# Feed-forward matmuls that read their moving operand in turns from two halves 1 KB apart

## The chip, the cores and the metric

The kernel runs on one core of a Trainium2 chip. The metric is the device time of one execution in microseconds (us), the median of three runs. A core has five engines that work side by side on their own instruction streams and wait for each other through semaphores: TensorE (PE in the profile; its weight loads are shown apart as PEld), VectorE (DVE), ScalarE (ACT), GpSimd (POOL) and SyncE (SP), which here only starts DMA transfers. SBUF is the memory on the core that the engines read, 128 partitions wide; PSUM takes the results of TensorE.

A matmul has two operands. The stationary one (128 partitions by 128 columns here) is put into the array by a weight load of its own. The moving one (128 partitions by 512 columns) is then streamed past it, column by column, and 128 x 512 results are added up in one bank of PSUM. The access pattern of the moving operand says in which order its 512 columns are read.

## The reference

An attention over 8 batches, 8 heads, 576 positions and 64 channels, in two parts that are added: a local one (each position sees those fewer than 4 away) and one on q, k and v averaged over groups of 4 positions, repeated for the four. The sum is laid out as 4608 tokens of 512 channels and goes through a feed-forward block, which is nearly all of the arithmetic:

```
h = x @ w_in                                  # 4608 x 512 @ 512 x 2048
g = where(h >= 1, h, where(h <= -1, 0, (h + 1)**2 / 4))
out = g @ w_out                               # 4608 x 2048 @ 2048 x 512
```

## The kernel before

**Feed-forward.** All numbers are float32. TensorE multiplies them in a rounded form (float32r), so each factor is split into a high part, which is the rounded number, and a low part, which is the rest; a product is made of three matmuls: high x high, high x low, low x high. The tokens are worked off in 9 chunks `c` of 512, the 2048 inner channels in 16 slices `f` of 128.

- `mm1(c, f)` (line 455) makes one slice of h for one chunk: 4 blocks `cc` of 128 channels, three matmuls each, so 12. Stationary is a 128 x 128 block of `w_in` (`wi[:, wt, ...]`, `wt` 0 for the high part and 1 for the low), moving are 512 tokens of `xh` or `xl` (line 466). Its result `h_ps` has channels on the partitions and tokens along the row. ScalarE, VectorE and GpSimd then apply the function and split the result into `gh` and `gl` (lines 476 to 485).
- `mm2(c, f)` (line 488) multiplies `g` with `w_out`: for each of 4 tiles `t` of 128 tokens three matmuls, so again 12. Stationary are 128 tokens of `gh` or `gl`, moving is a row of 512 columns of `wo` (line 500). The four banks `o_ps` add up over the 16 slices; after the last, ScalarE copies each to `osb` (line 504), and SyncE starts the transfer of its 128 rows of 512 floats to `out` (line 505).

There are 9 x 16 pairs of `mm1` and `mm2`, so 144 x 24 = 3456 feed-forward matmuls.

**Attention.** 32 pairs of heads, each in pieces that are put between the feed-forward matmuls. It writes the tokens into `xh` and `xl` (lines 358 and 359), a ring of 3 x 512 tokens for each of the 4 channel blocks.

**Weights.** `w_in` and `w_out` arrive in 16 + 16 transfers as 64-bit words (line 369) and are turned into the high and low float32r parts by ScalarE, VectorE and GpSimd (lines 381 to 390). On the host, `w_out` is only reshaped to 16 x 128 x 512 (line 555).

**Order.** Two lists of steps (lines 79 and 83) set the order of the first stage; after that, attention pieces, `mm1` and `mm2` take turns in a loop (line 511).

Of the kernel before, what the change touches and what calls it, by code (L numbers as in the profile page):

```python
# [17 lines left out]
P = 128  # L18
# [4 lines left out]
DM = H * D  # L23
# [3 lines left out]
NFC = DFF // P  # L27
TCH = 512
# [72 lines left out]
def attention_then_ffn(ctx: ExitStack, tc, qT, kT, vw, vp, band, w_in, w_out, out):  # L101
    nc = tc.nc
# [269 lines left out]
    def temp(name):  # L372
        return mpool.tile([P, 512], F32, name=name, tag="t512", bufs=4)
# [34 lines left out]
    def emit(op):  # L408
        kind, n = op[0], int(op[1:] or 0)
        if kind == "a":  # L410
            if n not in attentions:
                attentions[n] = attention(n, rot if n < NPAIR else ps_a)
            next(attentions[n], None)
        elif kind == "c":
            convert_weights(*next(todo["c"]))
        elif kind == "w":
            load_weights(next(todo["w"]))
        elif kind == "q":
            nc.sync.dma_start(qk[n][0], qT[0, n])
            nc.sync.dma_start(qk[n][1], kT[0, n])  # L420
        elif kind == "v":
            load(0, "vp")
            load(0, "v")
        elif kind == "s":
            mm1(*next(todo["s"]))
        elif kind == "m":
            mm2(*next(todo["m"]))
# [24 lines left out]
    gtiles = {}  # L452
    otiles = {}

    def mm1(c, f):
        r0 = (c % 3) * TCH
        ts = slice(r0, r0 + TCH)
        wi = weights["i", f]
        h = ps_h.tile([P, 512], F32, name="h_ps", tag="h")
        n = 0  # L460
        for cc in range(NCC):
            for wt, xt in ((0, xh), (1, xh), (0, xl)):
                nc.tensor.matmul(  # L463
                    h[:, :TCH],
                    wi[:, wt, cc * P : (cc + 1) * P],
                    xt[:, cc, ts],
                    start=(n == 0),
                    stop=(n == 3 * NCC - 1),
                )
                n += 1  # L470
        with tc.high_priority(offset=100):
            u = temp("u")[:, :TCH]


            if c == 0:
                nc.vector.tensor_scalar(u, h[:, :TCH], -1.0, 1.0, op0=ALU.max, op1=ALU.add)
                nc.scalar.activation(u, u, AF.Square, scale=0.5)
            else:
                nc.scalar.activation(u, h[:, :TCH], AF.Relu, bias=0.5, scale=0.5)  # L479
                nc.scalar.activation(u, u, AF.Square)  # L480
            nc.vector.scalar_tensor_tensor(u, h[:, :TCH], 1.0, u, op0=ALU.max, op1=ALU.min)  # L481
            gh = mpool.tile([P, TCH], F32R, name="gh", tag="gh", bufs=3)
            gl = mpool.tile([P, TCH], F32R, name="gl", tag="gl", bufs=3)
            nc.scalar.copy(gh, u)  # L484
            nc.gpsimd.tensor_tensor(gl, u, gh, op=ALU.subtract)  # L485
        gtiles[c, f] = gh, gl

    def mm2(c, f):
        gh, gl = gtiles.pop((c, f))
        if f == 0:  # L490
            otiles[c] = [
                ps_o.tile([P, 512], F32, name=f"o_ps{t}", tag=f"o{t}") for t in range(NTT)
            ]
        wo = weights["o", f]
        for t in range(NTT):
            o = otiles[c][t]
            ts = slice(t * P, (t + 1) * P)
            for n, (gt, wt) in enumerate(((gh, 0), (gh, 1), (gl, 0))):
                nc.tensor.matmul(  # L499
                    o, gt[:, ts], wo[:, wt, :], start=f == 0 and n == 0, stop=f == NFC - 1 and n == 2  # L500
                )
            if f == NFC - 1:
                osb = temp("osb")
                nc.scalar.copy(osb, o)
                nc.sync.dma_start(out[c * TCH + t * P : c * TCH + (t + 1) * P, :], osb)

    steps = [(c, f) for c in range(NCH) for f in range(NFC)]
    todo["s"], todo["m"] = iter(steps), iter(steps)
# [2 lines left out]
    for c, f in todo["s"]:  # L511

        attn_step(NPAIR * (c + 2))
        mm1(c, f)
        mm2(*next(todo["m"]))
    for c, f in todo["m"]:
        mm2(c, f)
# [52 lines left out]
```

## Time and profile before

| | |
|---|---|
| median of 3 runs | 996.58 us (995.63 to 997.15) |
| span of the profiled execution, first to last instruction | 993.5 us |
| what the median has beside that span | 3.1 us |
| PE busy | 965.2 us (97% of the span), 7036 instructions |
| PEld busy | 762.9 us (77%) |
| DVE, ACT, POOL busy | 382.5, 456.9, 369.4 us |
| DMA | 66.13 MB, mean 67 GB/s |

The profile gives the span of its own execution; its time from outside, as the runs are timed, is not recorded, so the 3.1 us are the difference to the median of other executions. Matmuls are pipelined: the record of one lasts some 390 ns and overlaps the next. What a matmul costs in a dense stream is therefore read from the distance between the starts of two that follow each other (the timeline), not from the mean of one in a group.

### The profile page before, as it was taken

To read this page: it belongs to the slowest core of one execution; us is meant where nothing else is said; L and a number is where in the kernel's file an instruction comes from. 1 tells how busy PE (TensorE), PEld (TensorE's weight loads), DVE (VectorE), ACT (ScalarE), POOL (GpSimd) and SP (SyncE) were. 2 spreads that over 40 slices of the span, in tenths; PEclk is the share of its full clock that TensorE was granted. 3 is DMA by queue.
4 is the path that set the end of the run, shared out by engine and by line. 5 is a ranking of instruction groups with operands and counts; after the bars stand their busy time and mean duration, and the time that the engine had idled before them with its cause. 6 is when DMAs were issued, how large, how long until landed. Compare 5 with 4: busy or idle time off the path is not lost.

```text
span 993.5 us, 16968 instructions
## 1 busy us (share of the span) xinstructions
PE 965.2 (97%) x7036; PEld 762.9 (77%) x7036; DVE 382.5 (39%) x644; ACT 456.9 (46%) x911; POOL 369.4 (37%) x309
## 2 busy tenths in 40 slices
PE   5699999999999999999999999999999999999998
PEld 4577777777777777777777777777777788888886
DVE  5877786333333333333333333333333311111110
ACT  4988444444454444444444345444444443334333
POOL 2547565343333333333333433333333322222222
PEclk8689999999999999999999999999999999999999
DMA  9685112111121112111211112111211010001001
GB/s 309 230 294 176 50 50 82 60 50 40 36 92 50 47 32 87 50 49 50 92 51 49 50 27 92 49 50 40 77 50 50 14 44 0 1 1 43 1 1 42
DMA packets 26524, 66.13 MB, mean 67 GB/s; under 512 B 3152, under 2 KB 3152, under 8 KB 26448
## 3 DMA queue, kind: packets, MB, share of 16 engines
q1 hardware_dynamic: 26448, 65.06, 20.1%
q8 instruction: 55, 0.90, 0.4%
q14 instruction: 21, 0.17, 0.1%
HBM read 55.61 MB, written 9.44 MB: 65 GB/s over the span
## 4 chain that ended last, share of the span: by engine, by line
PE 83%; issue 7%; POOL 3%; ACT 2%; DMA 2%; DVE 2%; SPq 0%; POOLq 0%; DVEq 0%; ACTq 0%
PE o_ps L499 36%; PE h_ps L463 36%; PE sl_ps L191 2%; PE pl_ps L324 2%; PE pl_ps L336 2%; PE tp_ps L292 2%; POOL gl L485 2%; PE sp_ps L226 2%; PE tl_ps L280 1%; DMA raw_i<-w_in 1%; DMA vp_sb<-vp 1%; DVE m L386 1%; DVE m L387 0%; ACT raw_i L381 0%; ACT w_i L389 0%
## 5 line engine op out<-in xcount | busy, mean ns | idle before, releaser
L463 PE MATMUL h_ps<-xh,w_i 128*128 128x512 f32 x1152 | 373.9, 402 | 0.0
L499 PE MATMUL o_ps<-w_o,gh 128*128 128x512 f32 x1152 | 360.1, 394 | 0.2
L485 POOL TENSOR_TENSOR gl<-u,gh 128x512 fp32r<-128x512 f32 x144 | 186.6, 1296 | 431.6 <-ACT gh L484 325.3
L481 DVE SCALAR_TENSOR_TENSOR u<-h_ps,u 128x512 f32<-128x512 f32 x144 | 99.5, 691 | 453.1 <-ACT u L480 450.3
L499 PEld LDWEIGHTS o_ps<-w_o,gh 128*128 128x128 f32 x1152 | 215.5, 188 | 48.9 <-ACT gh L484 1.0
L463 PEld LDWEIGHTS h_ps<-xh,w_i 128*128 128x128 f32 x1152 | 211.1, 188 | 48.1 <-issue 5.2
L499 PE MATMUL o_ps<-w_o,gl 128*128 128x512 f32 x576 | 229.4, 398 | 2.4 <-POOL gl L485 2.4
L463 PE MATMUL h_ps<-xl,w_i 128*128 128x512 f32 x576 | 226.8, 394 | 0.0
L479 ACT ACTIVATE u<-h_ps 128x512 f32<-128x512 f32 x128 | 76.3, 596 | 148.0 <-PE h_ps L463 148.0
L484 ACT CAST gh<-u 128x512 fp32r<-128x512 f32 x144 | 89.6, 622 | 104.7 <-DVE u L481 104.6
L499 PEld LDWEIGHTS o_ps<-w_o,gl 128*128 128x128 f32 x576 | 108.1, 188 | 33.0 <-issue 4.8
L463 PEld LDWEIGHTS h_ps<-xl,w_i 128*128 128x128 f32 x576 | 108.4, 188 | 24.0
L480 ACT ACTIVATE u<-u 128x512 f32<-128x512 f32 x128 | 80.9, 632 | 3.8
L273 POOL TENSOR_TENSOR vh<-vp_sb 72x512 f32<-72x512 f32 x28 | 36.4, 1301 | 102.0 <-ACT u L480 91.7
L218 ACT ACTIVATE sl<-sl 128x640 f32<-128x640 f32 x32 | 23.6, 737 | 105.3 <-POOL sl L217 105.3
L246 ACT ACTIVATE sp<-sp_ps,mxp 128x144 f32<-128x144 f32 x96 | 36.5, 380 | 35.2 <-DVE mxp L244 33.4
L359 POOL TENSOR_TENSOR xl<-x,xh 128x576 fp32r<-128x576 f32 (+2 forms) x40 | 47.4, 1192 | 6.3 <-ACT xh L358 6.2
L217 POOL TENSOR_TENSOR sl<-sl,mxl 128x640 f32<-128x640 f32 x28 | 35.5, 1268 | 31.1 <-DVE mxl L216 31.1
L284 ACT COPY al<-tl_ps 128x640 f32<-128x640 f32 x32 | 22.2, 694 | 52.1 <-PE tl_ps L280 52.1
L255 DVE TENSOR_REDUCE sp_ps<-sl 128x10 f32<-128x640 f32 x32 | 26.5, 827 | 42.8 <-ACT sp L246 42.8
L280 PE MATMUL tl_ps<-ident,sl 128*128 128x128 f32 x160 | 25.0, 290 | 15.2 <-DVE sl L258 15.2
L213 DVE TENSOR_TENSOR sl<-sl_ps,band_sb 128x640 f32<-128x640 f32 x28 | 23.1, 824 | 38.2 <-PE sl_ps L191 38.2
(67 smaller groups left out, 755.3 us busy)
## 6 DMA issues: line engine op xcount, KB each, us to landing
v_sb<-vw SPq DMA_DIRECT2D x32, 320.0 KB, 3.1
vp_sb<-vp SPq DMA_DIRECT2D x32, 288.0 KB
out<-osb SPq DMA_DIRECT2D x36, 256.0 KB, 2.2
raw_i<-w_in SPq DMA_DIRECT2D x16, 512.0 KB, 6.9
raw_o<-w_out SPq DMA_DIRECT2D x16, 512.0 KB, 7.7
q_sb<-qT SPq DMA_DIRECT2D x28, 288.0 KB, 2.9
k_sb<-kT SPq DMA_DIRECT2D x28, 288.0 KB, 8.8
first_i<-qT SPq DMA_DIRECT2D x4, 288.0 KB
```

Source lines behind the costliest of these rows:

```text
L217: nc.gpsimd.tensor_tensor(slf, slf, ml_n, op=ALU.subtract)
L246: nc.scalar.activation(sp[:, i], sp_v[:, i] if i < 2 else sp_w, AF.Exp, bias=mx[:, i : i + 1], scale=scale, accum_out=sums[:, NB + i : NB ...
L273: nc.gpsimd.tensor_tensor(vh, vpt[:, :, 0:2, :], vpt[:, :, 2:4, :], op=ALU.add)
L280: nc.tensor.transpose(tl_v[:, g * P : (g + 1) * P], sl[:, g].rearrange("p r c -> p (r c)"), ident)
L359: nc.gpsimd.tensor_tensor(xl[:, p, dst], x[:, part], xh[:, p, dst], op=ALU.subtract)
L463: nc.tensor.matmul(h[:, :TCH], wi[:, wt, cc * P : (cc + 1) * P], xt[:, cc, ts], start=(n == 0), stop=(n == 3 * NCC - 1),)
L479: nc.scalar.activation(u, h[:, :TCH], AF.Relu, bias=0.5, scale=0.5)
L480: nc.scalar.activation(u, u, AF.Square)
L481: nc.vector.scalar_tensor_tensor(u, h[:, :TCH], 1.0, u, op0=ALU.max, op1=ALU.min)
L484: nc.scalar.copy(gh, u)
L485: nc.gpsimd.tensor_tensor(gl, u, gh, op=ALU.subtract)
L499: nc.tensor.matmul(o, gt[:, ts], wo[:, wt, :], start=f == 0 and n == 0, stop=f == NFC - 1 and n == 2)
```

## The change

A helper `turns` takes a block of 512 columns as two halves of 256 and reads column 0 of the first half, column 0 of the second, column 1 of the first, column 1 of the second, and so on. A column is 4 bytes in each partition, so the two halves lie 1 KB apart. It is applied to the moving operand of both kinds of feed-forward matmul; the number of columns, the stationary operands and the results' places in PSUM are as before.

In `mm1`, the tokens thus come out of the matmul in turns from both halves of the chunk, and stay in that order through `u`, `gh` and `gl`. A tile of 128 rows of `o_ps` then holds 64 tokens of the first half and 64 of the second, and the transfer to `out` puts each row in its place. In `mm2` the columns of `w_out` are read in turns, and the host lays them out so that the results come in the right order.

```diff
+    def turns(x):
+
+        return x.rearrange("p (a b) -> p b a", a=2)
+
     def mm1(c, f):
...
                 nc.tensor.matmul(
                     h[:, :TCH],
                     wi[:, wt, cc * P : (cc + 1) * P],
-                    xt[:, cc, ts],
+                    turns(xt[:, cc, ts]),
                     start=(n == 0),
                     stop=(n == 3 * NCC - 1),
                 )
...
                 nc.tensor.matmul(
-                    o, gt[:, ts], wo[:, wt, :], start=f == 0 and n == 0, stop=f == NFC - 1 and n == 2
+                    o, gt[:, ts], turns(wo[:, wt, :]), start=f == 0 and n == 0, stop=f == NFC - 1 and n == 2
                 )
             if f == NFC - 1:
                 osb = temp("osb")
                 nc.scalar.copy(osb, o)
-                nc.sync.dma_start(out[c * TCH + t * P : c * TCH + (t + 1) * P, :], osb)
+                rows = out[c * TCH : (c + 1) * TCH, :].rearrange("(a b) d -> b a d", a=2)
+                nc.sync.dma_start(rows[t * P // 2 : (t + 1) * P // 2], osb)
...
-        "w_out": words(inputs["moe_w_out"]).reshape(NFC, P, DM),
+        "w_out": np.ascontiguousarray(
+            words(inputs["moe_w_out"]).reshape(NFC, P, DM // 2, 2).transpose(0, 1, 3, 2)
+        ).reshape(NFC, P, DM),
```

The instructions of every engine stand in the same order as before, and there are as many of each. Four lines are added ahead of `mm1`, so line 463 becomes 467 and line 499 becomes 503. Beside the matmuls' access patterns, only the form of the 36 output transfers differs. The rows below are from SyncE's order at the end of a chunk of tokens, with the change's row marked +:

```order
@@ -72,5 +72,5 @@
 L134 DMA q_sb<-qT 128x576
 L134 DMA k_sb<-kT 128x576
-L505 DMA out<-osb 128x512 x4
+L510 DMA out<-osb 64x2x512 x4
 L140 DMA v_sb<-vw 128x640
 L137 DMA vp_sb<-vp 72x1024
```

The four transfers stay in their place; each writes 64 pairs of rows, the two rows of a pair 256 rows apart in `out`, instead of 128 rows in a piece.

## The prediction

> **What bounds the kernel now.** I read the shares of the engines first, then the clock, then the windows, and last the distances between matmuls.
>
> ```profile
> PE 965.2 (97%) x7036; PEld 762.9 (77%) x7036; DVE 382.5 (39%) x644; ACT 456.9 (46%) x911; POOL 369.4 (37%) x309
> PEclk8689999999999999999999999999999999999999
> 0.00:50.00 50.00, 30.52 (x424) 24.25 (x424) 35.47 (x68) 33.21 (x76) 20.59 (x26) 0.74 0.78 270
> 50.00:100.00 50.00, 46.44 (x365) 35.30 (x364) 38.98 (x60) 41.67 (x83) 30.14 (x22) 0.92 0.66 232
> 100.00:150.00 50.00, 49.59 (x395) 39.01 (x395) 39.84 (x66) 24.18 (x49) 31.36 (x23) 1.00 0.17 50
> 150.00:200.00 50.00, 49.60 (x398) 38.93 (x397) 23.86 (x38) 22.79 (x44) 23.63 (x20) 1.00 0.22 70
> ...
> 300.00:400.00 100.00, 100.00 (x762) 78.69 (x762) 37.78 (x66) 44.87 (x92) 35.69 (x31) 1.00 0.18 57
> ```
>
> The second row is the granted clock of TensorE in 40 slices, and in the rows by window the columns are the window, its length, busy time of PE, PEld, DVE, ACT and POOL with counts, the granted clock, the DMA share and GB/s. From 100 us on the clock is full. TensorE is idle for 19.5 us in the first window, 3.6 in the second, 0.4 in each of the next two, and not at all between 300 and 400, where no other engine is busy half the time. So TensorE bounds the kernel nearly from end to end.
>
> A busy TensorE does not say what one matmul costs, since the records overlap. These are the groups of the feed-forward and the start times in a stretch without attention:
>
> ```profile
> L463 PE MATMUL h_ps<-xh,w_i 128*128 128x512 f32 x1152 | 373.9, 402 | 0.0
> L499 PE MATMUL o_ps<-w_o,gh 128*128 128x512 f32 x1152 | 360.1, 394 | 0.2
> L499 PE MATMUL o_ps<-w_o,gl 128*128 128x512 f32 x576 | 229.4, 398 | 2.4 <-POOL gl L485 2.4
> L463 PE MATMUL h_ps<-xl,w_i 128*128 128x512 f32 x576 | 226.8, 394 | 0.0
> ```
>
> ```profile
> 902.58 0.63 PE L463 MATMUL h_ps<-xh,w_i 128*128 128x512 f32 x2
> 903.05 0.39 PE L463 MATMUL h_ps<-xl,w_i 128*128 128x512 f32 x1
> ...
> 905.34 0.63 PE L499 MATMUL o_ps<-w_o,gh 128*128 128x512 f32 x2
> 905.81 0.40 PE L499 MATMUL o_ps<-w_o,gl 128*128 128x512 f32 x1
> ...
> 907.43 0.62 PE L499 MATMUL o_ps<-w_o,gh 128*128 128x512 f32 x2
> 907.88 0.39 PE L499 MATMUL o_ps<-w_o,gl 128*128 128x512 f32 x1
> 908.11 0.40 PE L463 MATMUL h_ps<-xh,w_i 128*128 128x512 f32 x1
> ```
>
> One `mm1` and one `mm2`, 24 matmuls, run from 902.58 to 908.11: 5.53 us, 230.4 ns from start to start, 0.45 ns a column. Two starting at 905.34 take 0.47 us, two at 907.43 take 0.45, so steps lie between 225 and 235 ns. The groups count 1152 + 1152 + 576 + 576 = 3456 matmuls; at 230.4 ns they are 796 us of the 993.5 us span. A nanosecond more on each is 3.5 us on the end.
>
> Each has a weight load of its own, and that is not what paces them:
>
> ```profile
> L463 PEld LDWEIGHTS h_ps<-xh,w_i 128*128 128x128 f32 x1152 | 211.1, 188 | 48.1 <-issue 5.2
> ```
>
> ```profile
> 608.20 0.71 PE L280 MATMUL tl_ps<-ident,sl 128*128 128x128 f32 x5
> 608.66 0.71 PE L463 MATMUL h_ps<-xh,w_i 128*128 128x512 f32 x2
> ```
>
> A load lasts 188 ns, 42 less than a step. In the attention, five matmuls of 128 columns with loads of the same size go from 608.20 to 608.66, 92 ns each by these merged starts. So loads can follow far faster than every 230 ns, and the 512 moving columns fill the step. What their reading costs more is paid in full.
>
> **The change part by part.** No instruction is added, removed or moved. Three things are different.
>
> (1) *The moving read of 3456 matmuls.* Before, neighbouring columns are read one after the other. Now each read is 1 KB from the one before, and none follows its neighbour. No matmul of the trace reads like this, so I bound the price. The nearest row is on another engine: line 268 adds up groups of four numbers that lie 512 bytes apart, lines 166, 242 and 243 reduce numbers that lie side by side.
>
> ```profile
> L268 DVE TENSOR_REDUCE vd<-vp_sb 72x256 f32<-72x1024 f32 x4 | 8.1, 2017 | 1.1 <-DMA vp_sb<-vp 0.8 <-PE pl_ps L336 0.3
> L166 DVE TENSOR_REDUCE first_qd<-q_sb 128x144 f32<-128x576 f32 x28 | 20.8, 741 | 0.3 <-DMA q_sb<-qT 0.3
> L242 DVE TENSOR_REDUCE sp_ps<-sp_ps 128x1 f32<-128x144 f32 x32 | 10.0, 313 | 14.5 <-PE sp_ps L226 14.5
> L243 DVE TENSOR_REDUCE sp_ps<-sp_ps 128x2 f32<-128x288 f32 x32 | 14.6, 456 | 0.1
> ```
>
> From 144 to 288 numbers the time grows by 143 ns, 0.99 ns each, with 170 ns fixed. Line 166, groups of four side by side, fits: (741 - 170) / 576 = 0.99. Line 268 gives (2017 - 170) / 1024 = 1.80 ns. Reading in turns from four places cost VectorE 0.81 ns a number, 0.82 of its own time for one.
>
> From below, the price on TensorE is nothing, or a gain; those are rivals. Where there is a stall, I scale it by the engine's own pace. The step of 225 ns is the most that streaming alone can be, since steps that short occur. At 0.82 of it a matmul costs 184 ns more; at a whole further column time for each column, 225 ns more. I take 213 ns, nearer the upper end: in line 268 each number still has a sum of four to close, in which a stall may hide, while a matmul has nothing between its columns. So 3456 x 213 = 736 us.
>
> [...]
>
> (2) *The order of columns and rows.* ScalarE, VectorE and GpSimd work on `u`, `gh` and `gl` element by element; the token order costs them nothing. `w_out` is laid out on the host, and its transfers are as large and as contiguous as before.
>
> (3) *The 36 output transfers.*
>
> ```profile
> out<-osb SPq DMA_DIRECT2D x36, 256.0 KB, 2.2
> ```
>
> Each still moves 128 rows of 2 KB and lands 2.2 us after its issue. All but the last lie under the matmuls. If the scattered rows doubled a landing, the end would come 2.2 us later; I count 0.
>
> *What takes some of it back.* A slower stream waits less for others. TensorE's idle time from 50 to 200 us is 4.4 us, and the groups show 2.4 us of waiting for `gl`. The first 19.5 us lie ahead of the feed-forward and stay. I count 4 us back. No engine becomes a bound: per feed-forward matmul all have the same work in nearly twice the time. As PE never rests, I expect the clock to stay full.
>
> *Sum.* The span of 993.5 becomes 993.5 + 736 - 4 = 1725.5, and with the 3.1 us that the median has beside it 1728.6: **1729 us**. With 184 and 225 instead of 213 it is 1629 and 1770, so the own range of this case is 1620 to 1780.
>
> **The rivals.**
>
> *No change (17%).* If the read addresses run far enough ahead of the array, a read elsewhere costs as little as a neighbour. For it: ScalarE reads every second word in line 381 at little extra over line 477, which reads all.
>
> ```profile
> L381 ACT ACTIVATE raw_i<-raw_i 128x512 f32<-128x512 f32 x16 | 10.7, 668 | 13.0 <-DMA raw_i<-w_in 13.0
> L477 ACT ACTIVATE u<-u 128x512 f32<-128x512 f32 x16 | 10.1, 630 | 7.4 <-DVE u L476 7.4
> ```
>
> 668 against 630 ns is 6%. Against it: its step is 8 bytes and not 1 KB, and line 268, with 512 bytes, shows that the distance is felt. The time would be 996.6. The same would show if the pattern had no effect on how the columns are fetched. [...]
>
> *Faster (22%).* If neighbouring reads meet in one part of the memory, and turns between two parts keep them out of each other's way, the steps become shorter. For it: they differ by 10 ns, though all do the same. With all at the shortest, 225 ns, 3456 x 5.4 = 19 us go and the time is 978; with the 10 ns once more below that, 215 ns, it is 943. It decides as soon as the mean step falls below 229.8 ns (2 us). Against it: line 268, which also takes turns between places 1 KB apart, is slower and not faster.
>
> *A stall on some reads only (7%).* One kind of matmul, or a read in four, pays: from 736 / 4 = 184 us to 368 us more, 1180 to 1365.
>
> *A stall that lasts as long as VectorE's (4%).* 0.81 ns on each of 512 columns is 415 ns a matmul and 1434 us in all: about 2430.
>
> **How the numbers follow.** The stall of nearly one column time has 50%, partial stalls 7%, the long one 4%: slower 61%. A measurement of this kernel can tell about 0.2% (2 us) from no change; the second rival lies inside that, 17%; faster 22%. The predicted time is that of the likeliest case, 1729 us. Cases of both signs hold most of the chance, so the range reaches from 950, into the faster case, to 1780, the likeliest case's upper end; it leaves out the long stall and the ends of the two. Between 1365 and 1620 I expect next to nothing.
>
> **What would show it.** Right: start to start of the matmuls at lines 467 and 503 near 443 ns on the timeline, in `mm1` and `mm2` alike; about 10.6 us for a pair of them where it was 5.53; PEld's share falling from 77% to near 45% with its loads still 188 ns; waits for `gl` gone; the attention matmuls unchanged; the granted clock still full. If `mm1` and `mm2` differ, the price hangs on what else lies in memory, not on the distance of 1 KB. Wrong: steps of 225 to 235 ns (no stall on TensorE, and VectorE's row was no guide), or steps under 225 (the reads were in each other's way before). If the steps double but the time does not, it was not TensorE that set the end. An output transfer that lands much later than 2.2 us would show the third part as mispriced.

## The result and the profile after

The changed kernel takes 954.36 us (median of 4 runs, 953.24 to 955.23), the kernel before 996.21 beside it. The ratio is 0.9577, 95% interval 0.9563 to 0.959: 4.2% faster, where 1729 us were predicted. The span of the profiled execution is 952.7 us, 40.8 less than before.

From the page of the changed kernel, shares of the engines, granted clock, and output transfers (KB each, us to landing):

```profile
PE 920.8 (97%) x7036; PEld 767.9 (81%) x7036; DVE 384.4 (40%) x644; ACT 459.4 (48%) x911; POOL 368.2 (39%) x309
PEclk7579999999999999999999999999999999999999
out<-osb SPq DMA_DIRECT2D x36, 256.0 KB, 2.5
```

The counts are those of before. TensorE is as busy as ever (97% of the span), its clock as full after the first slices (9 tenths or more), and the other engines have the same work. The transfers to `out` land 0.3 us later than the 2.2 of before. What changed is how fast matmuls follow each other. The timeline of the changed kernel, one `mm2` and one `mm1` (start, us, then the group):

```profile
900.22 0.59 PE L503 MATMUL o_ps<-w_o,gh 128*128 128x512 f32 x2
900.65 0.38 PE L503 MATMUL o_ps<-w_o,gl 128*128 128x512 f32 x1
...
902.80 0.59 PE L467 MATMUL h_ps<-xh,w_i 128*128 128x512 f32 x2
903.24 0.38 PE L467 MATMUL h_ps<-xl,w_i 128*128 128x512 f32 x1
...
905.39 0.59 PE L503 MATMUL o_ps<-w_o,gh 128*128 128x512 f32 x2
```

24 matmuls take 5.17 us where they took 5.53. Over all starts in the trace (steps next to attention left out) the mean step is 215.9 ns in both kinds, and in the dense stretch of the last two chunks nearly every one is 215 or 216. Before, the mean was 230.3 in `mm1` and 230.8 in `mm2`, and single steps went from 224 to 237 in a pattern that came back in each slice. Such means from the trace's starts are given for all runs below.

3456 x 14.7 ns would be 50.8 us; 40.8 arrived. The starts of `mm1` for each chunk say where the rest is. The first chunk begins at 55.9 us before and at 55.7 after, and then takes 109.7 us before and 111.6 after: it gained nothing. Chunks 1 to 6 take 5.3 us less each, chunks 7 and 8, which have no attention beside them, 5.6, which is 384 x 14.7 ns; from the start of the last matmul to the end of the span it takes 4.8 us instead of 4.3. In the windows of the first stage (window, length, busy PE, PEld, DVE, ACT, POOL, granted clock, DMA share, GB/s) of the changed kernel

```profile
50.00:100.00 50.00, 43.62 (x348) 33.93 (x347) 37.75 (x59) 45.41 (x82) 28.41 (x21) 0.88 0.65 230
100.00:150.00 50.00, 48.75 (x404) 40.00 (x403) 41.20 (x64) 23.62 (x47) 32.99 (x25) 1.00 0.17 50
150.00:200.00 50.00, 49.14 (x406) 40.35 (x405) 25.74 (x42) 23.61 (x47) 24.08 (x21) 1.00 0.22 70
```

TensorE idles 8.5 us between 50 and 200 us, where it idled 4.4, and the clock in the first of them is 0.88 instead of 0.92. In this stage the other engines convert weights and prepare attention; TensorE got to its waits sooner. That is read from the rows; no run changed this stage. The later traces agree with it: within the first chunk TensorE idles 2.9 us before, 5.0 with one kind of matmul turned, and 6.4 to 8.1 with both, and in none of them does the chunk take less than 109.7 us. The lower clock is not what they share: the changed kernel run again has 0.93 between 50 and 100 us, and its first chunk takes 111.7.

### The profile page after: what moved, and what is told of

Its sections match the earlier page's. It is cut to its first block, busy times and chain, and to the rows that moved or that the text cites. A ratio compares the mean times of both kernels' runs of the same rounds, so it can differ in the third digit from the quotient of the medians.

```text
span 952.7 us, 16968 instructions
## 1 busy us (share of the span) xinstructions
PE 920.8 (97%) x7036; PEld 767.9 (81%) x7036; DVE 384.4 (40%) x644; ACT 459.4 (48%) x911; POOL 368.2 (39%) x309
## 4 chain that ended last, share of the span: by engine, by line
PE 81%; issue 6%; ACT 5%; DVE 4%; POOL 2%; DMA 2%; SPq 0%; POOLq 0%; ACTq 0%; DVEq 0%
PE h_ps L467 34%; PE o_ps L503 34%; PE sl_ps L191 3%; PE pl_ps L324 2%; PE tp_ps L292 2%; PE pl_ps L336 2%; PE sp_ps L226 2%; PE tl_ps L280 2%; POOL gl L489 2%; DVE m L387 1%; DVE m L386 1%; ACT sp L246 1%; DMA raw_o<-w_out 1%; ACT raw_i L383 1%; ACT raw_i L381 1%
## 5 line engine op out<-in xcount | busy, mean ns | idle before, releaser
L467 PE MATMUL h_ps<-xh,w_i 128*128 128x512 f32 x1152 | 357.6, 388 | 0.1
L503 PE MATMUL o_ps<-w_o,gh 128*128 128x512 f32 x1152 | 345.2, 381 | 1.4 <-ACT gh L488 1.4
L503 PE MATMUL o_ps<-w_o,gl 128*128 128x512 f32 x576 | 222.1, 386 | 3.6 <-POOL gl L489 3.6
L467 PE MATMUL h_ps<-xl,w_i 128*128 128x512 f32 x576 | 218.8, 380 | 0.0
L467 PEld LDWEIGHTS h_ps<-xl,w_i 128*128 128x128 f32 x576 | 109.1, 189 | 14.7
L280 PEld LDWEIGHTS tl_ps<-ident,sl 128*128 128x128 f32 x160 | 19.5, 150 | 22.1 <-issue 13.3
```

The source lines that it names most:

```text
L280: nc.tensor.transpose(tl_v[:, g * P : (g + 1) * P], sl[:, g].rearrange("p r c -> p (r c)"), ident)
L467: nc.tensor.matmul(h[:, :TCH], wi[:, wt, cc * P : (cc + 1) * P], turns(xt[:, cc, ts]), start=(n == 0), stop=(n == 3 * NCC - 1),)
L503: nc.tensor.matmul(o, gt[:, ts], turns(wo[:, wt, :]), start=f == 0 and n == 0, stop=f == NFC - 1 and n == 2)
```

## The experiments

The question was why reading in turns is fast. Three theories: **parts**, two places far apart keep successive reads out of each other's way; **neighbours**, the straight read holds itself up by staying within a few bytes; **load**, the weight load of the next matmul and the straight read meet. My own theory, the lost turn (nearly a whole further column time for each column), was on the list too.

### One kind of matmul alone

`e1_mm1_only` keeps `turns` in `mm1` and reads `w_out` as before; `e2_mm2_only` the other way round:

```diff
-                    o, gt[:, ts], turns(wo[:, wt, :]), start=...
+                    o, gt[:, ts], wo[:, wt, :], start=...          # e1
-                    turns(xt[:, cc, ts]),
+                    xt[:, cc, ts],                                  # e2
```

> Only the moving operand of mm1 is read in turns; mm2 reads its 512 columns one after the other, and w_out is laid out as before. If the step of each turned matmul falls from 230.5 to 215.9 ns whatever stands beside it, mm1's 1728 matmuls bring 1728 x 14.6 = 25 us of 50, so about 21 of the 42 us measured: 975 us. If the two kinds disturb each other (a turned read helps the straight one behind it, or a straight one spoils the turned), the steps of mm2 fall below 230.8 ns too, or those of mm1 stay above 216, and the time is well off 975.

> Only the moving operand of mm2 is read in turns, with w_out laid out to match; mm1 and the output transfers are as before. Matmul by matmul: 975 us, steps of 215.9 ns in mm2 and 230.5 in mm1. The transfers' new form, if it costs anything, is missing here and there in the run with mm1 alone, so the two gains would add up to more than 42 us by that much.

Measured: 974.99 us, ratio 0.9793 (0.9774 to 0.9813), and 973.25 us, ratio 0.9778 (0.9763 to 0.9793). Timeline of the run with `mm1` alone:

```profile
851.13 0.61 PE L503 MATMUL o_ps<-w_o,gh 128*128 128x512 f32 x2
851.59 0.39 PE L503 MATMUL o_ps<-w_o,gl 128*128 128x512 f32 x1
...
852.49 0.59 PE L467 MATMUL h_ps<-xh,w_i 128*128 128x512 f32 x2
852.92 0.38 PE L467 MATMUL h_ps<-xl,w_i 128*128 128x512 f32 x1
```

Two straight matmuls take 0.46 us, two turned ones 0.43. In dense stretches the turned kind stands at 215.8 ns, the straight kind at 229 to 230. The gain belongs to each matmul by itself: 2.07% and 2.22% add up, within the intervals, to the 4.2% of both.

### Nine orders of the moving columns

`e3_scan_orders` gives each chunk of tokens another order, so that one run compares nine. This scan and the four like it are single runs; the steps are compared within the trace, not the times:

```diff
+    ORDERS = [
+        lambda x: x.rearrange("p (a b) -> p b a", a=2),             # chunk 0
+        lambda x: x,
+        lambda x: pairs_apart(x, 128), ... 64, 16, 4                # "p (x a b) -> p x b a", a=2
+        lambda x: x.rearrange("p (b a) -> p a b", a=2),             # 6
+        lambda x: x.rearrange("p (b a) -> p a b", a=4),
+        lambda x: x.rearrange("p (a b c) -> p b a c", a=2, c=4),    # 8
+    ]
```

> Each chunk of 512 tokens reads the moving operands of its 384 matmuls in another order (so the output is in a wrong order and partly a product of wrong columns; the work is the same). Chunk 0: turns 1 KB apart. 1: straight on. 2, 3, 4, 5: turns between places 512, 256, 64 and 16 bytes apart. 6: every second column, then the others (8 bytes apart). 7: every fourth (16 bytes apart). 8: four columns (16 bytes) from one half, then four from the other. Theory of parts (two places must lie in different parts of the memory, far apart): 215.9 ns in chunks 0 and 8 and from some distance on in 2 to 5; 230 ns or more in 1, 6, 7 and the short distances. Theory of neighbours (reads that stay within a few bytes hold each other up): 215.9 ns in 0, 2, 3, 4, 5 and 7, 230 in 1, something between in 6 and 8. Theory of the lost turn, which my prediction had (a read far from the last costs a further column time): 7 and 8 would be slower than 230.

The timeline of this run, a few rows each from chunk 1 (straight), 5 (turns 16 bytes apart), 6 (every second column) and 7 (every fourth):

```profile
200.56 0.62 PE L481 MATMUL h_ps<-xh,w_i 128*128 128x512 f32 x2
201.02 0.39 PE L481 MATMUL h_ps<-xl,w_i 128*128 128x512 f32 x1
...
640.38 0.59 PE L517 MATMUL o_ps<-w_o,gh 128*128 128x512 f32 x2
640.81 0.38 PE L517 MATMUL o_ps<-w_o,gl 128*128 128x512 f32 x1
...
741.08 1.09 PE L481 MATMUL h_ps<-xh,w_i 128*128 128x512 f32 x2
741.99 0.64 PE L481 MATMUL h_ps<-xl,w_i 128*128 128x512 f32 x1
...
920.95 1.10 PE L517 MATMUL o_ps<-w_o,gh 128*128 128x512 f32 x2
921.87 0.64 PE L517 MATMUL o_ps<-w_o,gl 128*128 128x512 f32 x1
```

Two steps take 0.46, 0.43, 0.91 and 0.92 us. Turns are at 215.8 to 216.1 ns at every distance, 16 bytes included: **parts** falls. Every fourth column, whose reads also lie 16 bytes apart, is at 460: **neighbours** falls as I had put it. And the lost turn exists: reading every second or fourth column costs 221 to 231 ns more than straight on. It does not come with turns.

### Sizes, loads and blocks

`e4_scan_forms` varies the operands' sizes by chunk:

```diff
+    FORMS = [(halves, P, TCH), (blocks(2), P, TCH), (blocks(16), P, TCH),
+        (lambda x: x[:, ::-1], P, TCH), (plain, P, 384), (halves, P, 384),
+        (plain, 72, TCH), (plain, P, TCH), (plain, 96, TCH)]
+        wgt = row[:, i::4] if c == 7 else row[:, i * P : (i + 1) * P]
```

> Again another form of the 384 matmuls in each chunk; after the first matmul of a sum, chunks 4 to 6 and 8 leave out part of the columns of one operand. Chunk 0: turns 1 KB apart, as control. 1 and 2: blocks of two and of 16 columns from the halves in turns. 3: straight on, but backwards. 4: 384 moving columns straight on. 5: 384 moving columns in turns. 6 and 8: straight on, with a stationary operand of 72 and of 96 columns instead of 128. 7: straight on, with a stationary operand whose columns lie 16 bytes apart. Theory of the load (the weight load of the next matmul and a straight moving read meet, 14.7 ns a matmul): the 14.7 ns shrink with the stationary columns, to 11 at 96 and 8 at 72 (steps of 227 and 224 ns), change in 7, and are the same 14 to 15 ns in 4 against 5. Theory of the read alone (the straight read holds itself up, whatever is loaded): 6, 7 and 8 stay at 230, and the difference of 4 and 5 is three quarters of 14.7, 11 ns. Backwards in 3: 230 if neighbours are what counts.

Weight loads of chunks 6 and 7, each from the groups of a window of that chunk (count, busy us, mean ns, idle):

```profile
L481 PEld LDWEIGHTS h_ps<-xh,w_i 128*72 128x72 f32 x64 | 9.0, 142 | 4.5
...
L481 PEld LDWEIGHTS h_ps<-xh,w_i 128*128 128x128 f32 x106 | 28.9, 308 | 0.0
```

With 72 stationary columns a load lasts 142 ns instead of 188, with columns 16 bytes apart 308; the steps are 231 to 233 ns with 72 columns, 231 to 234 with 96, 235 to 238 with the spread ones. A shorter load brings nothing, so **load** falls; a much longer one costs some 6 ns. With 384 moving columns in dense stretches, straight steps are 173 ns in `mm1` and 176 in `mm2`, turned ones 162.5 in both: 11 and 13 ns apart, where three quarters of 14.7 are 11. In `mm1` the loss thus goes with the number of columns read; in `mm2` it shrinks by less. Backwards: 233.6. Blocks from the two halves in turns are all slower than straight on: 334 ns with two columns, 240 with 16 (and 251 with four, in the run before).

### Two readers or kept lines

What turns of any distance have in common is that every second column of the order is a neighbour of the one two before. That led to the theory of two readers, one for even and one for odd positions in the order. No trace shows a reader; the theory is about the steps. `e5_scan_streams` tests orders in which it and its rivals part, and VectorE's row of my prediction beside it:

```diff
+    ORDERS = [halves, quarters, steps_of(2), steps_of(4),            # "p (a b e) -> p e b a", a=2
+        pairs_apart(x, 2), pairs swapped, 256 columns each twice, pairs_apart(x, 8), eighths]
-                vd, vpt.rearrange("k n f c -> k n c f"), axis=AX.X, op=ALU.add
+                dst, groups of four 512, 4, 16 or 8 bytes apart, axis=AX.X, op=ALU.add
```

> Another order of the moving columns in each chunk (the output is in a wrong order and partly a product of wrong columns). Chunk 0: halves in turns, as control. 1: quarters in turns (0, 128, 256, 384, 1, ...). 2: halves in turns, every second column of each (0, 256, 2, 258, ...), then the others. 3: the same with every fourth. 4: 0, 2, 1, 3, 4, 6, 5, 7, ... 5: neighbours swapped, 1, 0, 3, 2, ... 6: the first 256 columns, each twice in a row. 7: turns between places 32 bytes apart. 8: eighths in turns. Theory of two readers (even and odd columns are fetched by two readers, and each wants its next column in the 16 bytes it has just read; straight on, a reader finds two there, in turns four): 216 ns in 0, 6, 7; near 230 in 2, 4, 5, where each reader finds two; 330 to 460 in 1, 3, 8, where it finds one. Theory of kept lines (the last two or more 16-byte stretches are kept, and turns leave twice the time to fetch the next): 216 in 0, 6, 7 and, if four are kept, in 1; 230 in 4 and 5; 450 in 2, as where every second column was read straight on. Theory of 8-byte words: 216 in 4, 450 in 2. Beside it, line 268's reduction by VectorE takes its groups of four 512 bytes apart (as before), side by side, 16 bytes apart and 8 bytes apart, once each: if distance is what cost it 0.81 ns a number, 2.0, 1.2, 2.0 and 1.2 us.

Timeline, chunk 1 (quarters), 2 (halves, every second column), 3 (halves, every fourth), 6 (each column twice) and 8 (eighths):

```profile
220.68 0.73 PE L533 MATMUL o_ps<-w_o,gh 128*128 128x512 f32 x2
221.25 0.45 PE L533 MATMUL o_ps<-w_o,gl 128*128 128x512 f32 x1
...
340.44 0.62 PE L533 MATMUL o_ps<-w_o,gh 128*128 128x512 f32 x2
340.90 0.39 PE L533 MATMUL o_ps<-w_o,gl 128*128 128x512 f32 x1
...
480.18 1.08 PE L533 MATMUL o_ps<-w_o,gh 128*128 128x512 f32 x2
481.08 0.63 PE L533 MATMUL o_ps<-w_o,gl 128*128 128x512 f32 x1
...
870.60 0.59 PE L497 MATMUL h_ps<-xh,w_i 128*128 128x512 f32 x2
871.03 0.38 PE L497 MATMUL h_ps<-xl,w_i 128*128 128x512 f32 x1
...
1040.27 1.18 PE L497 MATMUL h_ps<-xh,w_i 128*128 128x512 f32 x2
1041.24 0.69 PE L497 MATMUL h_ps<-xl,w_i 128*128 128x512 f32 x1
```

All float32r orders of the runs together, sorted by how many successive reads of one reader fall into the same 16 bytes. The readers and the 16 bytes are the theory's assumptions; the steps are measured:

| order of the 512 columns | found together | step, ns (mm1 / mm2) |
|---|---|---|
| turns 1 KB, 512, 256, 64, 32 or 16 bytes apart | 4 | 215.8 to 216.2 |
| 256 columns, each twice | 4 | 215.8 / 215.8 |
| straight on | 2 | 230.2 / 230.6 |
| 0, 2, 1, 3, 4, 6, ... | 2 | 230.2 / 230.6 |
| neighbours swapped | 2 | 230.2 / 230.9 |
| halves in turns, every second column | 2 | 230.2 / 230.9 |
| backwards | 2 | 233.6 / 233.6 |
| blocks of 16; of 4 from the halves | 2 | 240.2 / 240.4; 249.9 / 251.9 |
| quarters in turns | 1 | 279.4 / 283.1 |
| blocks of 2 from the halves | 1 | 334.2 / 333.1 |
| every second; every fourth column | 1 | 454.3 / 451.8; 461.1 / 460.0 |
| halves in turns, every fourth column | 1 | 454.4 / 451.6 |
| eighths in turns | 1 | 487.5 / 487.5 |

Halves with every second column separate the theories. Kept lines and 8-byte words said 450; they are at 230 and repeat the pattern of straight steps (236, 235, 232, 232, 225, 230, ...). Halves with every fourth column are at 452 to 454, like every second column straight on. Each time it counts what lies at every second place of the order, not what lies next. **Two readers** sorts all fifteen into three classes without overlap. It does not give the sizes within a class: of the three orders forecast at 330 to 460, quarters came out below (279 to 283), eighths above (487). Quarters and blocks of two (334) come out cheaper than the other orders where a reader never finds two together. They alternate between two stretches a reader, eighths between four; so a stretch left for one read may still be at hand for the next. This stays open.

VectorE's four reductions in this run, with groups of four 512 bytes, 4, 16 and 8 bytes apart (start and us of each):

```profile
49.06 1.95 DVE L280 TENSOR_REDUCE vd<-vp_sb 72x256 f32<-72x1024 f32 x1 [1.05 <-PE tp_ps L302]
75.20 1.20 DVE L280 TENSOR_REDUCE vd<-vp_sb 72x256 f32<-72x1024 f32 x1
106.77 2.15 DVE L280 TENSOR_REDUCE vd<-vp_sb 72x256 f32<-72x1024 f32 x1
134.59 1.21 DVE L280 TENSOR_REDUCE vd<-vp_sb 72x256 f32<-72x1024 f32 x1
```

On VectorE distance does cost what I read from its row: 1.95 us at 512 bytes and 2.15 at 16, against 1.20 side by side. At 8 bytes it costs nothing (1.21 us), where on TensorE every second column, 8 bytes a step, doubles the time (452 to 454 ns against 230). TensorE's turns, at 16 bytes and more, are 14.7 ns a matmul faster than straight on.

### Other types of operand

`e6_scan_types` and `e9_scan_bf16` ask whether this carries over:

```diff
+    FORMS = [(halves, F32R), (plain, BF16), (halves, BF16), (every(2), BF16), (every(4), BF16),
+        (every(8), BF16), (every(16), BF16), (plain, F32), (halves, F32)]          # e6
+    FORMS = [(halves, F32R), plain, halves, each twice, blocks(2), apart(2), blocks(4),
+        apart(4), every(2), all BF16 with 256 columns]                             # e9
```

> Beside the first matmul of each sum, which stays as it was, chunks 1 to 6 use bfloat16 operands: one fixed stationary block and 256 fixed columns read twice (so the output is not the reference's), straight on in 1, halves (256 bytes apart) in turns in 2, every 2nd, 4th, 8th and 16th column in 3 to 6, which is 4, 8, 16 and 32 bytes from one to the next. Chunks 7 and 8 multiply the float32r tiles as plain float32, straight on and in turns; chunk 0 is in turns as control. By the theory of two readers a straight read of 2-byte columns finds four in each 16 bytes: 216 ns in 1 and 2, near 230 in 3, wait for each column (some 460) in 5 and 6, in 4 as well. By the theory of kept lines likewise 216 in 1 and 2, and 230 in 3. If only 4-byte operands are held up, 1 to 3 are alike. Plain float32 takes several passes; if a pass is slow enough for the reads, 7 and 8 are alike, and the attention's float32 matmuls have nothing to gain from turns.

> bfloat16 again, now 256 columns a matmul (one fixed stationary block and one fixed row of 256 columns beside the first matmul of each sum, so the output is not the reference's); straight on it should take half of 216, 108 to 110 ns. Chunk 1: straight on. 2: halves (256 bytes apart) in turns. 3: the first 128 columns, each twice. 4: blocks of two from the halves in turns. 5: 0, 2, 1, 3, ... 6: blocks of four from the halves. 7: 0, 4, 1, 5, ... 8: every second column, then the others. If two readers took even and odd columns here as well, 2, 3 and 7 would stand at 109; the 485 ns of the halves with 512 columns speaks against it. If the unit is a word of 4 bytes, two columns, then 4 takes the place of the turns (109) and 2, 3, 5 and 7, which break up the words, are slow (240). If a reader takes four columns at once from one 16-byte stretch, 1, 3, 5 and 6 are at 109 to 115, 2 and 4 near 240, 7 at 109 (eight neighbours in all), 8 at 113.

In the first, bfloat16 takes 216 ns straight on, 484 in turns of halves, 225 with every second column and 451 with every fourth. Every 8th and 16th are at 900 and 918, mostly at another clock. Windows of chunks 4, 5 and 6, then two short ones (the clock stands behind POOL), and matmuls of every 8th (`h_ps`) and every fourth column (`o_ps`) from there:

```profile
588.00:768.00 180.00, 180.00 (x794) 54.35 (x792) 36.23 (x60) 43.75 (x87) 38.45 (x35) 0.99 0.09 28
775.00:1130.00 355.00, 355.00 (x816) 72.34 (x816) 38.99 (x67) 45.67 (x90) 39.10 (x32) 0.51 0.05 15
1135.00:1500.00 365.00, 365.00 (x784) 74.28 (x783) 36.83 (x64) 47.27 (x94) 35.40 (x29) 0.50 0.03 11
...
764.00:774.00 10.00, 10.00 (x18) 2.08 (x17) 0.69 (x1) 2.60 (x5) 0.00 (x0) 0.50 0.07 26
774.00:780.00 6.00, 6.00 (x21) 1.26 (x20) 2.68 (x7) 2.71 (x9) 1.27 (x1) 1.00 0.35 131
```

```profile
759.54 10.06 PE L489 MATMUL h_ps<-half_x,ident 128*128 128x512 bf16 x11
769.42 5.59 PE L489 MATMUL o_ps<-half_x,ident 128*128 128x512 bf16 x12
...
775.92 10.06 PE L489 MATMUL h_ps<-half_x,ident 128*128 128x512 bf16 x11
```

The granted clock does not make these steps. Those of every 8th column take 900 ns at half clock and at full clock alike (from 776.80 to 780.40 us it is full), and the steps of every fourth from 769.42 us, at half clock, take 450 to 452 ns like those at full clock before. So at these two strides the steps took as long at half clock as at full. Columns 16 bytes apart cost bfloat16 900 ns, twice the 460 that they cost float32r, which no theory had forecast.

Plain float32 leaves two records for each matmul, here called passes. At the border of chunks 7 and 8, `mm1` (`h_ps`) already reads in turns and `mm2` (`o_ps`) still straight on:

```profile
1824.90 2.33 PE L498 MATMUL h_ps<-xh,w_i 128*128 128x512 f32 x4
1827.07 1.25 PE L498 MATMUL h_ps<-xl,w_i 128*128 128x512 f32 x2
1828.15 1.88 PE L498 MATMUL o_ps<-w_o,gh 128*128 128x512 f32 x4
1829.87 1.02 PE L498 MATMUL o_ps<-w_o,gl 128*128 128x512 f32 x2
```

A pass takes 429 ns straight on and 540 to 542 in turns, at full clock. Turns make plain float32 slower, by 111 to 113 ns a pass. That the attention's float32 matmuls would lose by them as well is my estimate from this; no run turned them.

In the second, with 256 columns, steps are 109 ns straight on, 109 with each column twice, with 0, 2, 1, 3 and with 0, 4, 1, 5; 113 with blocks of four and with every second column; 137 with blocks of two; 243 with halves. Rows from the straight order (chunk 1), the halves (chunk 2) and the blocks of two (chunk 4):

```profile
227.59 1.38 PE L492 MATMUL h_ps<-half_x,ident 128*128 128x256 bf16 x11
228.80 1.47 PE L492 MATMUL o_ps<-half_x,ident 128*128 128x256 bf16 x12
...
271.63 2.84 PE L492 MATMUL h_ps<-half_x,ident 128*128 128x256 bf16 x11
274.31 3.08 PE L492 MATMUL o_ps<-half_x,ident 128*128 128x256 bf16 x12
...
446.81 1.81 PE L492 MATMUL o_ps<-half_x,ident 128*128 128x256 bf16 x12
448.69 1.67 PE L492 MATMUL h_ps<-half_x,ident 128*128 128x256 bf16 x11
```

Two readers fails for bfloat16: halves should have been at 109. The third guess, that four successive columns are taken at once from one stretch of 16 bytes, fits seven of the eight orders and misses blocks of two (137 and not 240). What holds is practical: none of these orders beat bfloat16 operands read straight on (216 ns for 512 columns, 109 for 256), and turns between far halves more than double their time (484 and 243).

### Near turns in the whole kernel

`e7_turns_near` uses turns 256 bytes apart in `mm1` and 16 bytes apart in `mm2`; `e8_after_again` is the changed kernel on the same chip.

```diff
-        return x.rearrange("p (a b) -> p b a", a=2)
+        return x.rearrange("p (x a b) -> p x b a", a=2, b=b)     # b 64 in mm1, 4 in mm2
-                nc.sync.dma_start(rows[t * P // 2 : (t + 1) * P // 2], osb)
+                nc.sync.dma_start(rows.rearrange("(a b) d -> b a d", a=2), osb)
```

> The whole kernel with turns between near places: mm1 between tokens 256 bytes apart, mm2 between columns of w_out 16 bytes apart, tokens' rows and w_out laid out to match, so that each transfer to out again fills one piece of 128 rows. If distance does not matter, the same 215.8 ns and the same time as with turns 1 KB apart, beside it on the same chip, within 0.2%; if two parts of the memory 1 KB apart had a share in it, nearer to the kernel before.

> The changed kernel itself, to be compared with the near turns on the same chip: 954 us, ratio 0.958.

953.12 us, ratio 0.9574 (0.9556 to 0.9592), against 955.25 us, ratio 0.9588 (0.9572 to 0.9604). The mean steps are 215.8 to 215.9 ns in both, the intervals overlap, and the outputs land after 2.5 us here too. In the two profiles only the first chunk differs, 109.9 us against 111.7; why, stays open. The 1 KB has no share in the gain.

## Why the prediction was wrong

**What bounds the kernel** held. TensorE sets the end nearly throughout (busy 97% of the span before and after), and what was taken off each of the 3456 matmuls came off the time, except in the first chunk.

**Part (1), the price of the moving read**, failed, and with it the sum: +213 ns a matmul where -14.7 was measured. The 213 ns were my choice between the bounds, and no run shows them for these reads. The bounds from VectorE's row, 184 to 225 ns, happen to be near what other orders cost: reading every second or fourth column straight on costs 221 to 231 ns more. The wrong step was the sentence that each read is 1 KB from the one before and none follows its neighbour, so that all pay. Every column does follow its neighbour, two places later, and in the float32r orders measured here that is what counts: turns of any distance are at 215.8 to 216.2 ns, halves with every second column at 230, as straight on. VectorE's row told neither which orders pay nor how much: its own pattern, turns between four places 512 bytes apart, is that of quarters, which cost TensorE 49 to 53 ns more than straight on, not 184 to 225. (The 1 KB that a rival names for this row is the distance of every second place.)

**The step of 225 ns as the most that streaming can be** held as an upper bound, 9 ns too high: in the dense stretch of the changed kernel nearly every step is 215 or 216 ns and none is shorter. The spread of 225 to 235 ns, which I counted for a rival alone, went with the straight order; the turned steps do not have it. Where the clock is at 0.50 (55 to 58 us in both traces), the few straight and turned steps are alike, 426 to 427 ns (from 56.92 to 57.35 us before, from 56.70 to 57.13 after); in these traces the difference shows only at full clock. What streaming alone takes, no run shows; the shortest means for float32r are 215.8 ns for 512 columns and 162.5 for 384, 0.42 ns a column in both.

**Parts (2) and (3)** held: the other engines' times are as before, the transfers land 0.3 us later, and at the end of the kernel that is a few tenths of a microsecond (4.3 and 4.4 us after the last matmul's start with the old form, 4.7 and 4.8 with the new).

**What takes some of it back** had the wrong sign with the rest. I counted 4 us of waits that a slower stream would hide; a faster one met them earlier, and the first chunk grew by 1.9 us instead of shrinking by 5.6.

**The rivals.** The range held 954 us only because it reached down into a rival: faster (22%) is what happened, with its lower end of 215 ns and 943 us; 215.9 ns were reached, and the first chunk kept most of the 11 us between. Its mechanism, reads that meet in one part of the memory, does not fit the runs: turns 16 bytes apart do as well as turns 1 KB apart (215.8 to 216.2 ns). "No change" fell, as did the stalls: by their order alone, the same 512 columns took from 216 to 488 ns.

## What to carry to other kernels

Compare the distance between starts with the shortest that any order of the same columns reaches: a dense TensorE at 230 ns for 512 float32r columns lost 6% against the 215.8 ns of turns. Float32r operands read in turns from two places, even 16 bytes apart, took 215.8 to 216.2 ns, a gain if tokens or weight columns can be laid out for it at no cost. No order tried here beat bfloat16 or plain float32 operands read straight on (216 ns against 484 in turns of halves, 429 against 541 a pass). Reads that step evenly by 8 bytes or more took 452 to 461 ns with float32r (every second and fourth column) and 451 to 918 with bfloat16 (every fourth to every 16th): what to avoid with both. A price from another engine's row said neither which access patterns stall here nor how much (213 ns expected, -14.7 measured): measure the pattern on the engine that will use it.

## What was not expected of the hardware

- A straight float32r read is not the fastest: 230 ns against 215.8 for the same 512 columns.
- Every second column, 8 bytes a step, costs TensorE twice the time (452 to 454 ns against 230) and VectorE nothing (1.21 against 1.20 us).
- A stationary operand with columns 16 bytes apart makes its load 308 instead of 188 ns long, almost wholly hidden under the matmul: the steps are 235 to 238 ns instead of 230.
- Turns of halves, which speed float32r up, slow the others down: bfloat16 from 216 to 484 ns, plain float32 from 429 to 541 a pass.
- With every 8th and 16th bfloat16 column (steps of 900 and 918 ns) the granted clock fell to 0.51 and 0.50 although TensorE was busy without a gap (355.0 of 355 us, 365.0 of 365), and the steps of every 8th were as long at half clock as at full (900 ns).
